# A start-up rearranged: a differently split first conv, w_out's first quarter through SyncE, super 3's input queued early, another order of turns

## The chip, the cores and the metric

The kernel runs on one core of a Trainium2 chip. The metric is the device time in microseconds of one execution, here the median of several. Five engines work side by side: TensorE (PE, with its weight loads PEld), VectorE (DVE), ScalarE (ACT), GpSimd (POOL) and SyncE (SP). [...] DMAs are issued by POOL, ACT and SP, each with a queue of its own.

## The reference

`x` is (8, 4096, 192) f32, `weight` (8, 7), `w_in` (192, 2048), `w_out` (2048, 192). A causal depthwise conv of 7 taps, whose taps are a softmax for each of 8 heads, is followed by a two-layer network with ELU:

```python
w = softmax(weight, axis=-1)                        # (8 heads, 7 taps)
x_pad = concatenate([zeros((B, 6, D)), x], axis=1)
att[b, s, h, g] = sum_k w[h, k] * x_pad[b, s + k, h, g]
h = att.reshape(32768, 192) @ w_in                  # (32768, 2048)
g = where(h > 0, h, exp(minimum(h, 0)) - 1)
out = g @ w_out                                     # (32768, 192)
```

## The kernel before

**Tiling.** The 32768 tokens are 32 "supers" of 1024 tokens, and a super is two groups of 512 tokens, one for each half of TensorE's rows (r or g = 0, 1; 64 rows each, the two halves run side by side). The 192 channels are three tiles of 64 (j = 0, 1, 2). The 2048 hidden units are 16 blocks of 128 (q). A "unit" (n, r) is one hidden block of one group: three matmuls H (L1029) fill one PSUM bank of 128 x 512; ACT takes the exponential out of it into `E` (L756); POOL clips it to at most 1 (L710); DVE takes `max(E - 1, H)`, which is the ELU, into `gT` (L866) and so frees the bank. The second product O (L1052) then runs with gT as weights and `w_out` as the moving side, into accumulators that ACT copies to `osb` (L763), which SP stores. There are eight banks, shared by units, accumulators and convs.

**The conv.** For supers 1 to 31 it is a banded matmul (L1004): windows of x, loaded by POOL into `xg` (L627), times `Tm`, a band of taps; ACT copies the result to `csb` (L752), and SP transposes it by DMA into `att` (L608). `Tm` is made once: DVE writes `wband` (L822), SP writes it to DRAM as `conv_band` (L1075), waits for that to land, and reads it back with a skewed pattern (L1084).

**The first super** takes another way, since nothing is loaded yet. ACT loads all its x to `xs` by one DMA; PE transposes it (L936), ACT and DVE copy it to `xT` (L740, L830), and a conv of tap matmuls (L978) makes the three parts of `att`: each matmul is a diagonal of taps, 64x64, times xT shifted by the tap. Four such 64x64 quarters of TensorE can run at once: the tiles j = 0 and j = 2 use the two diagonal quarters, j = 1 the other two. Of tile 0's seven taps, `ON_DVE` = 3 are done on DVE instead (L837, L842) and added at the end (L849). Tile 2 is done in two halves of 256 columns, in two banks; ACT copies the first to `att` (L744), DVE the second (L851). Only then do the first H matmuls run.

**Weights.** POOL's queue issues, in this order: `w_in` in two column halves of three DMAs each (L647; cast to bf16 on the way), the first piece of `w_out` (L658, blocks 0 to 3, cast to fp16 on the way), both groups of x of super 1 (L627), two more pieces of w_out (blocks 4 to 7, 8 to 15), both groups of x of super 2, and the first group of x of super 3; then its clips begin. The second group of super 3 is issued before clip number 48 (`X3_AT`). `w_in` lands on partitions 0 to 63 and is copied to 64 to 127 for the other row half: ACT copies two parts (L734) and DVE two (L854) from the first column half, ACT a third one later, and SP the rest by DMA (L1092).

**Order.** PE's order is planned while the program is built: `live` (L232) runs the first 16 hidden blocks through a model of the engines (constants `ACT_H`, `POOL_H`, `DVE_H`, `TURNS`, times `LANDS` at which loads are there, `UPPER_LATE` at which the second row half may begin) and always issues what can begin first; `emit` (L189) merges fixed lists after that. The order is a list that PE follows strictly: a matmul whose semaphore has not come holds everything behind it. ACT's and DVE's orders follow from PE's. The engines' own instruction streams are in order too.

The core of the merge of the first conv, and the wait that each O matmul has on its piece of w_out:

```python
rows_of = [
    [(0, tap, 0, GS, 0) for tap in range(KSIZE - ON_DVE)]
    + [(2, t, GS // 2 * c, GS // 2 * (c + 1), 2 + c) for c in range(2) for t in range(KSIZE)],
    [(1, tap, 0, GS, 1) for tap in range(KSIZE)],
]
...
W(s_w[2 + next(k for k in range(1, 4) if q < WOUT[k])], 16)
```

Of the kernel before, what the change touches and what calls it, by code (L numbers as in the profile page):

```python
# [6 lines left out]
ACT = mybir.ActivationFunctionType  # L7
# [3 lines left out]
FP32 = mybir.dt.float32  # L11
# [23 lines left out]
O_AT = (12, 16)  # L35
CONV_AT = (14, 18, 22, 26)
CONV_POS = ((4, 4), (4, 4), (4, 4), (4, 4))
POS_FROM = 19
QB = 2
WARM = (8, 1, 4)  # L40
WCOLS = ((0, 8 * FC), (8 * FC, 16 * FC))
UPPER = ((0, FC), (FC, 2 * FC), (2 * FC, 4 * FC), (4 * FC, 8 * FC), (8 * FC, 16 * FC))
WOUT = (0, 4, 8, 16)
X3_AT = (0, 48)
HALO = 8
BW = P
ON_DVE = 3
XL = GS - CW * (NWIN - 1) + PAD
XI = SUP // P
MM_H, MM_O, MM_C = 216.0, 82.5, 102.5  # L50
# [7 lines left out]
LATE_Q, COPY_AT = 9, 6  # L58
LIVE, UNTIL = 16, 20
EARLY_O = (4, 8)  # L60
LANDS = {"x": {1: 7200.0, 2: 14200.0}, "w_in": 10200.0, "w_out": (3900.0, 8400.0, 11000.0)}
DONE_PE, TO_ACT, TO_POOL, TO_DVE, TO_PE = 165.0, 40.0, 85.0, 35.0, 60.0
ACT_H, ACT_C, ACT_O, POOL_H, DVE_H = 495.0, 470.0, 390.0, 578.0, 600.0
ENDS_ACT, ENDS_POOL, ENDS_DVE, TRANSPOSED = 103.0, 37.0, 84.0, 5000.0
TURNS = 320.0
X_AT = ((2, 1, 1), (1, 1, 0))
ZERO_AT = 8
TAIL = 18
UPPER_LATE = 600.0


def bass_lightweight_conv__then__act_elu_kernel(
# [159 lines left out]
    def live(last, convs, turns):  # L232
# [26 lines left out]
        def o_ready(rt, g):  # L259
            if not turns[rt][g]:  # L260
                return far
            k, q0, q1, visit, *_ = turns[rt][g][0]
            if visits.get((k, g), 0) != visit:
                return far
            t = max(gt_at.get((NQ * (k // 2) + q, g), far) for q in range(q0, q1))
            if k < 2:
                t = max(t, LANDS["w_out"][next(i for i in range(3) if q1 <= WOUT[i + 1])])
            if visit == 0:
                return max(t, min(freed))
            return max(t, turned[k, g])  # L270
# [143 lines left out]
    with ExitStack() as stack:  # L414
# [39 lines left out]
        block8 = sbuf("block8", [HEADS, HEADS, KSIZE], BF16)  # L454
        wband = sbuf("wband", [P, HEADS + 1, BW], BF16)
        scr = sbuf("scr", [P, 2], FP32)
        H = psum("H", [P, NBANK, GS])

        s_wq = sema("s_wq")
# [8 lines left out]
        s_xs = sema("s_xs")  # L468
        s_xh = sema("s_xh")
        s_wb = sema("s_wb")  # L470
        s_xz = sema("s_xz")
        s_cast = sema("s_cast")
        s_tap = sema("s_tap")
# [51 lines left out]
        def att_need(s):  # L525
# [7 lines left out]
            ("t", 3): (0, 2),  # L533
            ("d", 0): (0, 3),
            ("d", 1): (3, 0),
            ("d", 2): (4, 4),
        }

        def first_evacuated(W, what):
# [74 lines left out]
        def _gpsimd(g: bass.BassGpSimd):  # L614
# [78 lines left out]
            ).then_inc(s_id)  # L693
            load_w_in(0)
            load_w_in(1)
            load_w_out(0)
            for gr in range(2):
                load_x(1, gr)
            load_w_out(1)
            load_w_out(2)  # L700
            for gr in range(2):
                load_x(2, gr)
            for i, (n, u) in enumerate(units):
# [15 lines left out]
        @block.scalar  # L719
        def _scalar(a):  # L720
            W = Waits(a)
            a.dma_start(
                xs[:, :, :], x_flat[0:SUP, :].rearrange("(p i) d -> p i d", i=XI)
            ).then_inc(s_xs, 16)
            a.memzero(scr[:, 0:1]).then_inc(s_scr)  # L725
            W(s_scr, 1)
            a.activation(scr[:, 1:2], scr[:, 0:1], ACT.Exp)
            W(s_set, 2)
            a.activation(wex[:], wq2[:], ACT.Exp).then_inc(s_wex)
            W(s_xs, 16)  # L730
            for j in (0, 2):
                a.activation(*cast(j), ACT.Copy).then_inc(s_cast)  # L732
            def upper_half(c0, c1):
                a.activation(  # L734
                    w_in[HP:P, :, c0:c1], w_in[0:HP, :, c0:c1], ACT.Copy
                ).then_inc(s_wa)

            for j in range(1, 3):
                W(s_xt, 2 * j)
                a.activation(*transposed(j), ACT.Copy).then_inc(s_fa)  # L740
            W(s_first[1], 1)
            a.activation(*first_att(1, 0, GS), ACT.Copy).then_inc(s_fa)
            W(s_first[2], 1)
            a.activation(*first_att(2, 0, GS // 2), ACT.Copy).then_inc(s_fa)  # L744
            W(s_w[0], 48)
            for k in range(2):
                upper_half(*UPPER[k])
            for item in act_order:
                if item[0] == "c":
                    m = item[1]  # L750
                    W(s_cv, m + 1 - CU)
                    a.activation(*conv_evac(W, m), ACT.Copy).then_inc(s_ce)  # L752
                elif item[0] == "h":
                    i = unit_at[item[1:]]
                    W(s_h, i + 1)
                    a.activation(  # L756
                        E[:, i % NE, :], H[:, bank_of[item], :], ACT.Exp
                    ).then_inc(s_exp)
                    if i == COPY_AT:
                        W(s_w[1], 48)  # L760
                        upper_half(UPPER[4][0], FC * LATE_Q)
                else:
                    a.activation(*out_evac(W, *item[1:]), ACT.Copy).then_inc(s_oev[item[2]])  # L763
            evacuated_by(W, NK - 1, 1)
            out_group(a, NK - 1, 1)

        @block.vector
        def _vector(v):
# [79 lines left out]
            to, at = first_att(0, 0, GS)  # L848
            v.tensor_tensor(to, at, part[:], ALU.add).then_inc(s_fd)  # L849
            W(s_first[3], 1)  # L850
            v.tensor_copy(*first_att(2, GS // 2, GS)).then_inc(s_fd)  # L851
            W(s_w[0], 48)
            for c0, c1 in UPPER[2:4]:
                v.tensor_copy(w_in[HP:P, :, c0:c1], w_in[0:HP, :, c0:c1]).then_inc(s_wc)  # L854
            for item in dve_order:
                if item[0] == "e":
                    v.tensor_copy(*out_evac(W, *item[1:])).then_inc(s_od)  # L857
                    continue
                _, n, u = item
                i = unit_at[n, u]  # L860
                s, q = divmod(n, NQ)
                if s >= NG3:
                    for g in range(2):
                        W(s_fin[g], 2 * (s - NG3 + 1))
                W(s_clp, i + 1)
                v.scalar_tensor_tensor(  # L866
                    out=gT[:, s % NG3, q, u, :],
                    in0=E[:, i % NE, :],
                    scalar=1.0,
                    in1=H[:, bank_of[item], :],  # L870
                    op0=ALU.subtract,
                    op1=ALU.max,
                ).then_inc(s_tt)

        @block.tensor
        def _tensor(pe):
# [19 lines left out]
            for item in pe_order:  # L896
# [58 lines left out]
                elif item[0] == "d":  # L955


                    rows_of = [
                        [(0, tap, 0, GS, 0) for tap in range(KSIZE - ON_DVE)]
                        + [(2, t, GS // 2 * c, GS // 2 * (c + 1), 2 + c) for c in range(2) for t in range(KSIZE)],  # L960
                        [(1, tap, 0, GS, 1) for tap in range(KSIZE)],
                    ]
                    merged, ends = [], [0, 0]
                    while any(rows_of):
# [6 lines left out]
                    for j, tap, c0, c1, which in merged:  # L971
# [2 lines left out]
                            W(s_tap, 3)  # L974
                        last = KSIZE - 1 - (ON_DVE if j == 0 else 0)
                        for r in range(2):
                            rows, to = half_of(r), half_of(r ^ (j == 1))
                            ins = pe.matmul(  # L978
                                H[to, bank_of["d", j] + (j == 2 and c0 > 0), c0:c1],
                                taps[rows, tap, rows],  # L980
# [58 lines left out]
                else:  # L1039
# [6 lines left out]
                        wait_bank(("a", k, g))  # L1046
                    if visit is not None and not opens:
                        W(s_turn[g], turns[k, g])
                    W(s_w[2 + next(k for k in range(1, 4) if q < WOUT[k])], 16)
                    W(s_tt, tt_count(NQ * t + q, g))  # L1050
                    t0 = 2 * P * half + P * kb
                    ins = pe.matmul(  # L1052
# [14 lines left out]
        def _sync(sy):  # L1067
# [3 lines left out]
                weight[:, :],  # L1071
            ).then_inc(s_wq, 16)
            sy.dma_start(xh[:, :], x_flat[GS - HALO : GS, :]).then_inc(s_xh, 16)
            W(s_tap, 3)
            sy.dma_start(  # L1075
                bass.AP(
# [57 lines left out]
```

## Time and profile before

| what | value |
|---|---|
| median of 4 runs | 718.27 us (718.07 to 718.58) |
| profiled execution | 718.58 us, its span 716.8 us |
| granted TensorE clock | 1.00 throughout |
| H matmuls (L1029) | 3072, 64x512 each |
| O matmuls (L1052) | 8192, 64x192 each |
| banded conv (L1004) | 496, 64x240 each |
| gT on DVE (L866) | 1024, mean 682 ns |
| clip on POOL (L710) | 1024, mean 614 ns |
| exponential on ACT (L756) | 1024, mean 601 ns |
| HBM read, written | 34.63 MB, 25.46 MB |

The time of the profiled execution is 1.8 us more than its span, which begins with the program's first instruction. A mean duration is longer than the spacing of instructions that follow each other, since the next one starts before the last has drained: clips of 614 ns mean start some 575 ns apart. "Busy" for PE means that at least one matmul is in its pipeline, so a stage in which PE is busy all the time can still hold far fewer matmuls than another; the counts of the stages tell that.

### The profile page before, as it was taken

How to read it: one execution, taken by the hardware profiler on the slowest of the kernel's cores; microseconds unless marked ns; L12 is line 12 of the kernel's file. 1: busy time of each engine (PE TensorE's matmuls, PEld its weight loads, DVE VectorE, ACT ScalarE, POOL GpSimd, SP SyncE). 2: the span in 40 equal slices, each digit the busy share in tenths (PEclk: the TensorE clock that was granted, in tenths of full speed). 3: DMA queues.
4: the chain of work that ended last, by engine and by line, in shares of the span. 5: the costliest groups of instructions: out<-in, count | busy, mean ns of one | idle time of the engine just before them, and what ended most of it. 6: DMA issues, size and time to landing. Idle time of an engine off the chain costs nothing.

```text
span 716.8 us, 27665 instructions
## 1 busy us (share of the span) xinstructions
PE 710.8 (99%) x11875; PEld 681.8 (95%) x11875; DVE 642.0 (90%) x1048; ACT 677.3 (95%) x1290; POOL 663.7 (93%) x1112
## 2 busy tenths in 40 slices
PE   8999999999999999999999999999999999999998
PEld 4689999999999999999999999999999999999998
DVE  7999899998898998899998989988989988999994
ACT  6999999999999999999999999999999999999994
POOL 9999999999999999999999999999999999999893
PEclk9999999999999999999999999999999999999999
DMA  9635334564443554444654344544445534434212
GB/s 185 97 72 93 67 73 77 93 87 75 80 80 74 94 90 64 77 86 80 87 90 71 72 77 95 87 73 77 84 73 91 93 63 76 89 81 84 58 48 69
DMA packets 132303, 58.80 MB, mean 82 GB/s; under 512 B 98374, under 2 KB 131412, under 8 KB 132180
## 3 DMA queue, kind: packets, MB, share of 16 engines
q0 software_dynamic: 43504, 16.77, 22.7%
q1 hardware_dynamic: 88388, 39.37, 22.3%
q8 instruction: 93, 1.52, 0.9%
q10 hardware_dynamic: 288, 0.88, 0.4%
q14 instruction: 30, 0.25, 0.1%
HBM read 34.63 MB, written 25.46 MB: 84 GB/s over the span
## 4 chain that ended last, share of the span: by engine, by line
PE 96%; POOL 2%; ACT 1%; DVE 0%; issue 0%; DVEq 0%; POOLq 0%
PE H L1052 54%; PE H L1029 37%; PE H L1004 4%; POOL xg L627 1%; ACT E L756 1%; POOL w_in L647 1%; POOL E L710 1%; POOL w_out L658 0%; DVE gT L866 0%; ACT csb L752 0%; POOL owner L675 0%; DVE osb L857 0%; POOL block L685 0%; POOL ident L664 0%; POOL ones L662 0%
## 5 line engine op out<-in xcount | busy, mean ns | idle before, releaser
L866 DVE SCALAR_TENSOR_TENSOR gT<-E,H 128x512 f16<-128x512 f32 x1024 | 631.9, 682 | 62.1 <-POOL E L710 57.6
L1029 PE MATMUL H<-att,w_in 64*128 64x512 bf16 x3072 | 679.8, 376 | 1.4 <-DVE gT L866 1.0
L1052 PE MATMUL H<-w_out,gT 64*128 64x192 f16 x8192 | 680.5, 243 | 0.1
L710 POOL TENSOR_SCALAR E<-E 128x512 f32<-128x512 f32 x1024 | 603.1, 614 | 41.2 <-ACT E L756 34.3
L1052 PEld LDWEIGHTS H<-w_out,gT 64*128 64x128 f16 x8192 | 606.4, 94 | 17.7 <-PE H L1052 1.5
L756 ACT ACTIVATE E<-H 128x512 f32<-128x512 f32 x1024 | 585.0, 601 | 24.0 <-PE H L1029 0.5
L1029 PEld LDWEIGHTS H<-att,w_in 64*128 64x128 bf16 x3072 | 275.7, 93 | 7.6 <-DVE gT L866 3.0
L1004 PE MATMUL H<-xg,Tm 64*128 64x240 bf16 x496 | 90.9, 263 | 0.0
L752 ACT ACTIVATE csb<-H 112x480 bf16<-112x480 f32 x124 | 70.7, 570 | 0.5 <-PE H L1004 0.3
L763 ACT ACTIVATE osb<-H 128x384 f32<-128x384 f32 (+1 forms) x129 | 62.0, 482 | 6.9 <-PE H L1052 6.8
L627 POOL DMA_DIRECT2D xg<-in_x_dram x62 | 55.0, 900 | 0.2 <-issue 0.2
L1004 PEld LDWEIGHTS H<-xg,Tm 64*128 64x128 bf16 x496 | 42.6, 94 | 1.2 <-DVE gT L866 0.3
L857 DVE COPY osb<-H 128x192 f32<-128x192 f32 x1 | 0.4, 357 | 7.3 <-PE H L1052 7.3
L903 PE MATMUL H<-const-bfloat16-1.0 128*128 128x512 bf16 x12 | 4.5, 535 | 0.8 <-PEq L1119 0.8
L903 PEld LDWEIGHTS H<-const-bfloat16-1.0 128*128 128x128 bf16 x12 | 1.3, 124 | 2.8 <-issue 2.5
L647 POOL DMA_DIRECT2D w_in<-in_moe_w_in_dram x6 | 3.8, 660 | 0.0
L732 ACT ACTIVATE xb<-xs 128x512 bf16<-128x512 f32 x2 | 1.1, 621 | 2.4 <-DMA xs<-in_x_dram 2.4
L658 POOL DMA_DIRECT2D w_out<-in_moe_w_out_dram x3 | 3.0, 1058 | 0.0
L978 PE MATMUL H<-xT,taps 64*64 64x256 bf16 (+1 forms) x50 | 2.6, 317 | 0.0
L978 PEld LDWEIGHTS H<-xT,taps 64*64 64x64 bf16 x50 | 2.0, 106 | 0.5
L725 ACT ACT_TABLE_LOAD x1 | 1.3, 1283 | 1.2 <-PEq L1119 1.2
L936 PEld LDWEIGHTS H<-ident,xb 64*64 64x64 bf16 x48 | 1.2, 127 | 1.3 <-ACT xb L732 1.2
(44 smaller groups left out, 20.9 us busy)
## 6 DMA issues: line engine op xcount, KB each, us to landing
out_dram<-osb SPq DMA_DIRECT2D x126, 192.0 KB, 2.9
xg<-in_x_dram POOLq DMA_DIRECT2D x61, 240.0 KB, 4.6
xs<-in_x_dram ACTq DMA_DIRECT2D x1, 768.0 KB, 4.6
w_in<-in_moe_w_in_dram POOLq DMA_DIRECT2D x6, 128.0 KB, 4.3
att<-csb SPq DMA_TRANSPOSE x31, 3.9
w_out<-in_moe_w_out_dram POOLq DMA_DIRECT2D x2, 192.0 KB, 7.9
w_out<-in_moe_w_out_dram POOLq DMA_DIRECT2D x1, 384.0 KB, 11.8
w_in<-w_in SPq DMA_DIRECT2D x1, 336.0 KB, 6.7
```

The costliest lines, as they stand in the source:

```text
L627: g.dma_start(xg[0:rows, b, 2 * w0 + gr : 2 * w1 : 2, :], src).then_inc(s_x[b][gr], 16)
L647: g.dma_start(w_in[0:HP, j, c0:c1], bass.AP(tensor=moe_w_in.tensor, offset=8 * j * FF + c0, ap=[[CPH * FF, HEADS], [FF, 8], [1, c1 - c0]], ...
L710: g.tensor_scalar(out=E[:, i % NE, :], in0=E[:, i % NE, :], scalar1=1.0, scalar2=0.0, op0=ALU.min, op1=ALU.max,).then_inc(s_clp)
L752: a.activation(*conv_evac(W, m), ACT.Copy).then_inc(s_ce)
L756: a.activation(E[:, i % NE, :], H[:, bank_of[item], :], ACT.Exp).then_inc(s_exp)
L763: a.activation(*out_evac(W, *item[1:]), ACT.Copy).then_inc(s_oev[item[2]])
L866: v.scalar_tensor_tensor(out=gT[:, s % NG3, q, u, :], in0=E[:, i % NE, :], scalar=1.0, in1=H[:, bank_of[item], :], op0=ALU.subtract, op1=A ...
L903: pe.matmul(H[:, bank, :], nc.const_aps.tensor(1.0, (P, P), BF16), nc.const_aps.tensor(1.0, (P, GS), BF16), start=True, stop=True,)
L978: ins = pe.matmul(H[to, bank_of["d", j] + (j == 2 and c0 > 0), c0:c1], taps[rows, tap, rows], xT[rows, j, HALO - PAD + tap + c0 : HALO - P ...
L1004: ins = pe.matmul(H[:, bank_of["c", m], 256 * q : 256 * q + UC], Tm[rows, h, :], xg[rows, s % NXB, :, CPH * h : CPH * (h + 1)].rearrange(" ...
L1029: ins = pe.matmul(H[:, bank_of[item[:3]], :], w_in[HP * r : HP * (r + 1), j, FC * q : FC * (q + 1)], att[HP * r : HP * (r + 1), s % 2, j, ...
L1052: ins = pe.matmul(acc_of(k, g)[:, D * kb : D * (kb + 1)], gT[HP * rt : HP * (rt + 1), t % NG3, q, g, t0 : t0 + P], w_out[HP * rt : HP * (r ...
```

## The change

Six edits, all in the first 50 us of the kernel:

- The first conv: two taps on DVE instead of three; tile 2 is cut at column 352 (`SPLIT`) instead of 256, and its last 160 columns run on the quarters of tile 1 (so its row halves arrive swapped, and DVE copies them back in two instructions of 64 rows).
- ACT's two copies of w_in's upper half come before its copies of `att`, not after.
- w_out's blocks 0 to 3 are loaded by SP as f32 into a new buffer `wo`, after x has landed and ahead of `conv_band`; DVE casts them into `w_out` after its two w_in copies and ahead of its first gT. O matmuls of these blocks wait for the cast (`s_wo`). Blocks 4 to 15 come as one DMA by POOL.
- Both groups of super 3's x are issued before POOL's first clip.
- Constants of the planner: landing times, POOL_H and DVE_H, TURNS, and UPPER_LATE from 600 to 1200.
- `POS_FROM`: the convs of blocks 17 and 18 take the later positions too.

```diff
-POS_FROM = 19
+POS_FROM = 17
-WOUT = (0, 4, 8, 16)
-X3_AT = (0, 48)
+WOUT = (0, 4, 16)
+X3_AT = (0, 0)
-ON_DVE = 3
+ON_DVE = 2
+SPLIT = 352
-LANDS = {"x": {1: 7200.0, 2: 14200.0}, "w_in": 10200.0, "w_out": (3900.0, 8400.0, 11000.0)}
+LANDS = {"x": {1: 7200.0, 2: 14200.0}, "w_in": 10200.0, "w_out": (3600.0, 9700.0)}
-ACT_H, ACT_C, ACT_O, POOL_H, DVE_H = 495.0, 470.0, 390.0, 578.0, 600.0
+ACT_H, ACT_C, ACT_O, POOL_H, DVE_H = 495.0, 470.0, 390.0, 570.0, 590.0
-TURNS = 320.0
+TURNS = 250.0
-UPPER_LATE = 600.0
+UPPER_LATE = 1200.0
...
             load_w_in(0)
             load_w_in(1)
-            load_w_out(0)
             for gr in range(2):
                 load_x(1, gr)
             load_w_out(1)
-            load_w_out(2)
...
+            W(s_w[0], 48)
+            for k in range(2):
+                upper_half(*UPPER[k])
             W(s_first[1], 1)
             a.activation(*first_att(1, 0, GS), ACT.Copy).then_inc(s_fa)
             W(s_first[2], 1)
-            a.activation(*first_att(2, 0, GS // 2), ACT.Copy).then_inc(s_fa)
-            W(s_w[0], 48)
-            for k in range(2):
-                upper_half(*UPPER[k])
+            a.activation(*first_att(2, 0, SPLIT), ACT.Copy).then_inc(s_fa)
...
-            v.tensor_copy(*first_att(2, GS // 2, GS)).then_inc(s_fd)
+            to, at = first_att(2, SPLIT, GS)
+            for g in range(2):
+                v.tensor_copy(
+                    to[HP * g : HP * (g + 1), :], at[HP * (1 - g) : HP * (2 - g), :]
+                ).then_inc(s_fd)
             W(s_w[0], 48)
             for c0, c1 in UPPER[2:4]:
                 v.tensor_copy(w_in[HP:P, :, c0:c1], w_in[0:HP, :, c0:c1]).then_inc(s_wc)
+            W(s_w[3], 16)
+            v.tensor_copy(w_out[:, 0 : WOUT[1], :], wo[:, :, :]).then_inc(s_wo)
...
-                        + [(2, t, GS // 2 * c, GS // 2 * (c + 1), 2 + c) for c in range(2) for t in range(KSIZE)],
-                        [(1, tap, 0, GS, 1) for tap in range(KSIZE)],
+                        + [(2, tap, 0, SPLIT, 2) for tap in range(KSIZE)],
+                        [(1, tap, 0, GS, 1) for tap in range(KSIZE)]
+                        + [(2, tap, SPLIT, GS, 3) for tap in range(KSIZE)],
...
-                            rows, to = half_of(r), half_of(r ^ (j == 1))
+                            rows, to = half_of(r), half_of(r ^ (which % 2))
...
-                    W(s_w[2 + next(k for k in range(1, 4) if q < WOUT[k])], 16)
+                    if q < WOUT[1]:
+                        W(s_wo, 1)
+                    else:
+                        W(s_w[4], 16)
...
             sy.dma_start(xh[:, :], x_flat[GS - HALO : GS, :]).then_inc(s_xh, 16)
+            W(s_xs, 16)
+            sy.dma_start(
+                wo[:, :, :],
+                moe_w_out.rearrange("(q p) d -> p q d", p=FC)[:, 0 : WOUT[1], :],
+            ).then_inc(s_w[3], 16)
             W(s_tap, 3)
```

## The prediction

> **What bounds the kernel now.** I read the page first. TensorE is busy for 99% of the span at the full granted clock, and matmuls are 91% of the chain that ended last.
>
> ```profile
> span 716.8 us, 27665 instructions
> PE 710.8 (99%) x11875; PEld 681.8 (95%) x11875; DVE 642.0 (90%) x1048; ACT 677.3 (95%) x1290; POOL 663.7 (93%) x1112
> PE H L1052 54%; PE H L1029 37%; PE H L1004 4%; POOL xg L627 1%; ACT E L756 1%; POOL w_in L647 1%; POOL E L710 1%; POOL w_out L658 0%; DVE gT L866 0%; ACT csb L752 0%; POOL owner L675 0%; DVE osb L857 0%; POOL block L685 0%; POOL ident L664 0%; POOL ones L662 0%
> ```
>
> Busy time hides the start-up, so I read the busy time by stage next (each engine's busy us with its count of instructions in brackets; PE is the first).
>
> ```profile
> 24.00:28.00 4.00, 3.95 (x40) 2.16 (x37) 3.62 (x6) 4.00 (x10) 3.43 (x6) 1.00 0.27 49
> 28.00:32.00 4.00, 4.00 (x47) 2.35 (x46) 4.00 (x8) 3.93 (x9) 3.92 (x8) 1.00 0.43 68
> 36.00:40.00 4.00, 4.00 (x62) 3.35 (x62) 3.86 (x7) 3.87 (x9) 3.76 (x7) 1.00 0.15 49
> 60.00:80.00 20.00, 20.00 (x344) 19.17 (x339) 18.50 (x31) 19.27 (x38) 18.87 (x33) 1.00 0.43 83
> ```
>
> From 60 us on PE finishes 344 matmuls in 20 us, 69 per 4 us; between 24 and 32 us it is called busy too, yet finishes 40 and 47. So PE is the bound only from about 36 us. Before that it is another engine; the timeline of the first microseconds names the chain that starts it (start, duration, then in brackets the idle time and its releaser).
>
> ```profile
> 5.93 1.12 POOL L658 DMA_DIRECT2D w_out<-in_moe_w_out_dram  x1
> 6.72 2.04 POOL L627 DMA_DIRECT2D xg<-in_x_dram  x2
> 8.55 1.84 POOL L658 DMA_DIRECT2D w_out<-in_moe_w_out_dram  x2
> 10.17 2.78 POOL L627 DMA_DIRECT2D xg<-in_x_dram  x3
> 12.78 1.41 POOL L710 TENSOR_SCALAR E<-E 128x512 f32<-128x512 f32 x2
> 13.64 2.48 DVE L866 SCALAR_TENSOR_TENSOR gT<-E,H 128x512 f16<-128x512 f32 x4 [1.03 <-POOL E L710]
> 14.39 1.49 PE L1029 MATMUL H<-att,w_in 64*128 64x512 bf16 x7 [0.87 <-DVE gT L866]
> ```
>
> The first exponential on ACT runs from 11.45 for 0.60 us, so E is there at 12.05; POOL is still writing DMA descriptors and clips it only at 12.78. DVE starts its gT at 13.64, and PE, out of banks, waits 0.87 us. After that VectorE alone, in the windows of L866, is busy 21.94 of 22.5 us from 13.5 to 36 us: it makes 40 gT at some 0.6 us each, back to back. A shift of its first gT is therefore a shift of everything up to 36 us, and from there PE carries the same shift to the end. Two other places matter: SyncE's queue, and a hole at 43 us.
>
> ```profile
> 6.77 0.37 SPq L1075 DMA_DIRECT2D conv_band<-wband  x1
> 12.67 0.35 SPq L1084 DMA_DIRECT2D Tm<-conv_band  x1
> conv_band<-wband SPq DMA_DIRECT2D x1, 288.0 KB, 5.9
> Tm<-conv_band SPq DMA_DIRECT2D x1, 256.0 KB, 5.6
> 19.26 0.26 PE L1004 MATMUL H<-xg,Tm 64*128 64x240 bf16 x1
> 42.80 0.89 POOL L627 DMA_DIRECT2D xg<-in_x_dram  x1
> 44.38 1.88 DVE L866 SCALAR_TENSOR_TENSOR gT<-E,H 128x512 f16<-128x512 f32 x3 [0.76 <-POOL E L710]
> 45.12 0.39 PE L1029 MATMUL H<-att,w_in 64*128 64x512 bf16 x1 [0.18 <-DVE gT L866]
> ```
>
> Tm lands at 12.67 + 5.6 = 18.3 and the first banded conv reads it at 19.26: 1.0 us of slack. At 42.80 POOL issues the second half of super 3's x; VectorE stands 0.76 us and PE 0.18 us.
>
> [...] the two copies of L854, bf16 in SBUF, take 0.67 and 1.19 us beside POOL's descriptor writing[...] DMA is over 90% busy from 4 to 9 us, and conv_band, 288 KB, needs 5.9 us there. [...]
>
> **The change part by part.** The sums are against the profiled execution, 718.58 us with a span of 716.8; the median is 718.27, and I carry the difference over to it.
>
> *POOL's queue.* Spacings of starts: w_out's first piece 6.72 - 5.93 = 0.79; two xg 1.83; two w_out 10.17 - 8.55 = 1.62, so 0.83 for eight blocks; three xg to the first clip 2.61. Sum 6.85. After: two xg 1.83, one piece of twelve blocks 0.87 (the slope from four to eight), four xg 4 x 0.87 = 3.48, sum 6.18. POOL is free at 5.93 + 6.18 = 12.1, just as E is ready: gain up to 0.65 us at the first clip.
>
> *VectorE's queue.* One tap less: -0.75 (L842). The 128x256 copy (0.42) becomes two of 64x160, 0.3 each by that row: +0.2. L854 then ends near 12.4 instead of 12.61. New after it: wait for wo, then cast 768 columns. wo is issued near 5.5, once xs has landed (ACT's first read of it is at 5.46). Landing: conv_band's 5.9 or the first w_out's 7.3 us later, so 11.4 to 12.8; I take 12.4. Everything on VectorE, so every gT, queues behind this wait. The cast: 0.72 us by scaling L814 (512 columns in 0.48)[...]; I take 0.6. If it does not collide, gT starts at 12.1 + 0.83 + 0.05 = 13.0, or at 13.0 by VectorE's own queue. If cast and clip exclude each other, 12.1 + 0.83 + 0.6 = 13.55. [...] I take 13.55: gain 0.1, bounds +0.6 and -0.3.
>
> *First conv.* Each diagonal pair has 5 x 512 + 7 x 352 = 5024 columns instead of 4 x 512 + 7 x 512 = 5632; 608 columns at 216 ns per 512 (PE's spacing) end it 0.26 us sooner, at 10.1. But the first H needs all three parts of att, and ACT now makes two w_in copies first (L734, 0.93 us). The third w_in transfer, issued at 3.8, lands near 9.2, so the copies end at 10.1, att(1) at 10.65 and 352 columns of att(2) at 11.05; the third H started at 10.97 before. Gain nothing: the copies that stood after att now stand before it.
>
> *SyncE's queue.* wo (128 x 4 x 192 x 4 B = 393 KB) now lies ahead of conv_band. The same bytes crossed the same engines at that time before, so the least cost is nothing; the most is its own passage at the 200 GB/s of 10 to 12 us, 2.0 us. I take 0.8: Tm lands near 19.1, inside the slack. At 2.0 the first conv would wait 1.0 to 1.1 us with all H and O behind it. xl and w_in's upper half (lands near 21.0) move as much; its first reader, unit 9, runs at 22.2, so it is covered when Tm is.
>
> *w_out's rest.* Twelve blocks now land as one, about when the last piece did (9.3 + 11.8 = 21.1). O of q = 4 stood 76th in PE's order and stands 91st, which before was at 21.2. Cost 0 to 0.5; I take 0.1.
>
> *Super 3's x.* The issue at 42.80 goes. VectorE's hole of 0.76 closes; PE's visible idle is 0.18 us, its first O after it a little later too: gain 0.3 (0.2 to 0.4). Its transfer is now queued with the others, up to some 25 us, where the transpose of att (issued 25.82) may share engines with it; H of super 1 starts at 30.9, a microsecond after that transpose lands.
>
> *Order of turns.* From the middle of unit 18 to the end all engines' orders are the same, bank numbers apart; the steady state and the tail are not touched.
>
> Sum: -0.1 - 0 + 0.1 - 0.3 = -0.3 us: 718.3 for the profiled one, 718.0 on the median.
>
> **The rivals.**
> - [...] gT starts at 13.0: -0.6 - 0.3 = -0.9, with a shorter startup order up to -1.4: 716.9 to 717.4. For it: E is ready at 12.05 and POOL at 12.1. Against: the slow L854 copies.
> - *The SyncE queue decides.* wo delays Tm by 2.0 us or more and w_in's upper half with it: first conv +1.1 to +1.8, gT +0.3 for a late wo, -0.3 for the hole: 719.4 to 720.1, slower. It decides from 1.0 us of delay on. For it: conv_band already needs 5.9 us for 288 KB. Against: those bytes were in the way before.
> - *VectorE waits for wo.* Tm in time, but wo at 13.2, as w_out's first piece (5.93 + 7.3): gT at 13.9 to 14.2: +0.3 to +0.6 - 0.3 + 0.1: 718.4 to 718.7.
>
> **How the numbers follow.** Likeliest case 0.47 (718.0, its own range 717.4 to 718.6), no collision 0.2, SyncE's queue 0.2, wo late 0.13. 0.2% is 1.44 us, about what a measurement of this kernel tells from no change: limits 716.83 and 719.71. Only the far end of the second case (0.12) and most of the third (0.16) lie outside. Range 716.8 to 719.7.
>
> **What would show it.** POOL's first clip near 12.2; first gT at 13.0 (no collision), 13.55 or 13.9; VectorE idle before the w_out cast, if wo is late; conv_band and Tm landings, and idle PE before the first L1004 matmul; no VectorE hole at 43 us; 344 matmuls in 60 to 80 us again. A change of that last count would make the whole argument wrong.

## The result and the profile after

| | before | after |
|---|---|---|
| median | 718.30 us (62 runs, 718.01 to 719.34) | 721.32 us (42 runs, 718.62 to 724.77) |
| ratio, 95% interval | | 1.0045, 1.0036 to 1.0054: 0.45% slower, beyond the noise |
| profiled execution, its span | 718.58 us, 716.8 us | 718.85 us, 716.9 us |

The median stands where hardly any execution is: the 42 times of the changed kernel lie in two groups of 21, from 718.6 to 720.8 and from 721.9 to 724.8 us, most of the second above 723.3. The kernel before, run beside it, has no second group (62 runs up to 719.34). The mean granted clock splits the same way: it is 0.999 or 1.00 in every run of the lower group and 0.993 to 0.998 in every run of the upper one. The profiled execution belongs to the lower group; a profile of the upper one came from running the same kernel again (724.51 us, span 722.7 us). The two are the same program, so what differs between them is most of the loss. A smaller part is in both: the lower group's median, 719.25 us, is already 0.95 us above that of before, and the profiled 718.85 is among its fastest.

The ratios here and below lie near the quotient of the mean times, not of the medians. With two groups these can differ: in `e1_again`, below, the means give 1.0049 and the medians 1.0070.

First the windows view of the changed kernel in its lower execution, then in its upper one (the columns are the stretch, its length, each engine's busy us with its count of instructions, PE first, then PEld, DVE, ACT, POOL, the granted clock, the DMA share and GB/s).

```profile
12.00:16.00 4.00, 4.00 (x30) 1.40 (x26) 3.74 (x7) 3.92 (x8) 3.66 (x7) 1.00 1.51 217
16.00:20.00 4.00, 3.91 (x42) 2.09 (x40) 4.00 (x7) 3.81 (x8) 4.00 (x8) 1.00 1.41 250
20.00:24.00 4.00, 3.99 (x49) 2.52 (x46) 3.71 (x7) 3.77 (x8) 3.27 (x6) 1.00 1.53 206
24.00:28.00 4.00, 4.00 (x52) 2.66 (x47) 3.33 (x7) 4.00 (x9) 3.16 (x7) 1.00 0.64 97
60.00:80.00 20.00, 20.00 (x341) 19.35 (x338) 18.47 (x30) 19.31 (x37) 18.87 (x33) 1.00 0.44 84
80.00:100.00 20.00, 20.00 (x344) 19.49 (x341) 18.12 (x30) 19.24 (x38) 18.80 (x32) 1.00 0.48 88
```

```profile
12.00:16.00 4.00, 1.84 (x14) 0.61 (x11) 1.77 (x1) 3.95 (x8) 4.00 (x8) 0.99 1.51 215
16.00:20.00 4.00, 2.59 (x11) 0.88 (x11) 4.00 (x7) 1.24 (x3) 1.65 (x3) 0.50 1.51 221
20.00:24.00 4.00, 3.84 (x28) 2.00 (x28) 3.34 (x7) 1.80 (x4) 2.02 (x4) 0.50 1.43 235
24.00:28.00 4.00, 4.00 (x43) 2.81 (x40) 2.20 (x4) 2.73 (x7) 2.02 (x4) 0.73 0.39 46
60.00:80.00 20.00, 20.00 (x342) 19.43 (x337) 18.01 (x30) 19.24 (x38) 19.12 (x33) 1.00 0.50 88
```

Between 12 and 28 us PE finishes 30 + 42 + 49 + 52 = 173 matmuls in the one and 14 + 11 + 28 + 43 = 96 in the other, and VectorE makes 28 instructions against 19. From 60 us on they keep the same pace (341 and 342 matmuls in 60 to 80 us, 344 before). The loss is made before 28 us, and a part of it at half the clock. The timeline of VectorE says where it starts; the first two lines are the lower execution, the next two the upper one, and the last one of each fence is the first gT.

```profile
12.98 0.56 DVE L861 CAST w_out<-wo 128x768 f16<-128x768 f32 x1 [0.26 <-DMA wo<-in_moe_w_out_dram]
13.47 1.27 DVE L873 SCALAR_TENSOR_TENSOR gT<-E,H 128x512 f16<-128x512 f32 x2
```

```profile
14.23 2.52 DVE L861 CAST w_out<-wo 128x768 f16<-128x768 f32 x1 [2.33 <-DMA wo<-in_moe_w_out_dram]
16.68 3.66 DVE L873 SCALAR_TENSOR_TENSOR gT<-E,H 128x512 f16<-128x512 f32 x6
```

The same cast of 768 columns, waiting for the same transfer: in one execution wo lands at 12.96 and the cast takes 0.56 us; in the other it lands at 14.21 and the cast takes 2.52. The first gT stands behind it. PE has filled its banks by then in the upper execution (2 + 22 H matmuls, three to each of eight banks):

```profile
10.87 2.96 PE L1038 MATMUL H<-att,w_in 64*128 64x512 bf16 x22 [0.17 <-DVE att L854]
17.41 2.31 PE L1038 MATMUL H<-att,w_in 64*128 64x512 bf16 x8 [3.57 <-DVE gT L873]
```

PE idles for 3.57 us, and the clock records show 0.5 from 15.91 for 10.24 us. In the lower execution PE has no gap above 0.25 us between 11 and 24 us and no such record. At 718.58 + 3.04 (the first gT at 16.68 instead of 13.64) the upper execution would be at 721.6; the other 2.9 us of its 724.51 follow with the halved clock.

SyncE's queue shows the second effect, in the DMA issues of the lower execution (KB, then us from issue to landing):

```profile
wo<-in_moe_w_out_dram SPq DMA_DIRECT2D x1, 384.0 KB, 7.4
conv_band<-wband SPq DMA_DIRECT2D x1, 288.0 KB, 7.1
Tm<-conv_band SPq DMA_DIRECT2D x1, 256.0 KB, 5.2
```

conv_band takes 7.1 us where it took 5.9, and lands at 14.03 instead of 12.66; Tm lands at 19.26 instead of 18.28. The first banded conv starts at 19.30, on Tm's heels.

### The profile page after: what moved, and what is told of

Same layout as the page of the kernel before. It is cut to its first block, busy times and chain, and to the rows that moved or that the text cites. A ratio compares the mean times of both kernels' runs of the same rounds, so it can differ in the third digit from the quotient of the medians.

```text
span 716.9 us, 27669 instructions
## 1 busy us (share of the span) xinstructions
PE 712.6 (99%) x11877; PEld 681.4 (95%) x11877; DVE 642.0 (90%) x1049; ACT 677.9 (95%) x1290; POOL 663.1 (92%) x1110
## 4 chain that ended last, share of the span: by engine, by line
PE 97%; DVE 2%; ACT 0%; issue 0%; POOL 0%; DVEq 0%
PE H L1064 55%; PE H L1038 37%; PE H L1013 4%; DVE gT L873 1%; PE H L910 1%; ACT E L757 0%; DVE part L838 0%; ACT csb L753 0%; DVE xT L831 0%; DVE part L843 0%; PE H L943 0%; DVE att L850 0%; POOL E L711 0%; DVE osb L864 0%; PE H L920 0%
## 5 line engine op out<-in xcount | busy, mean ns | idle before, releaser
L987 PE MATMUL H<-xT,taps 64*64 64x512 bf16 (+2 forms) x52 | 2.3, 319 | 0.0
```

The lines of the kernel that those rows point to most:

```text
L987: ins = pe.matmul(H[to, bank_of["d", j] + (j == 2 and c0 > 0), c0:c1], taps[rows, tap, rows], xT[rows, j, HALO - PAD + tap + c0 : HALO - P ...
```

## The experiments

No kernel below leaves out a part of the computation; some write a buffer that nothing reads, and say so. A row of the later table is one profiled execution, while times and ratios are medians over all runs of a kernel.

### Which part of the change loses the time

`e1_again` is the changed kernel as it is.

> The changed kernel again, to see whether its times stay spread between 718.6 and 724.8 us in two groups (about 719.2 and 724), and to have a second profile of it. Theory X3 (the early transfer of super 3's second x group runs into the first transpose of att): two groups again, and a profile from the upper group would show the first H of super 1 some 5 us late behind L611's transpose. Theory W (twelve blocks of w_out as one transfer land with no slack before O of q = 4): two groups too, but the 5 us stand before that O, near 22 us. Theory T (Tm late behind wo): the 5 us stand before the first L1013 matmul, near 19 us.

723.67 us (718.99 to 724.99), ratio 1.0048 (1.0031 to 1.0064). It repeats the loss and the two groups, ten of 17 runs above 722, and gave the upper profile shown above. None of the three places that the theories name is where the time is lost: that is ahead of the first gT.

`e1_no_wo` has everything of the change except wo:

```diff
+            load_w_out(0)
...
-            W(s_w[3], 16)
-            v.tensor_copy(w_out[:, 0 : WOUT[1], :], wo[:, :, :]).then_inc(s_wo)
...
-            W(s_xs, 16)
-            sy.dma_start(
-                wo[:, :, :],
...
```

> The changed kernel with w_out's blocks 0 to 3 loaded by POOL with a cast as before (first after w_in), no wo, no cast on DVE, SyncE's queue as before. Theory T: the upper group vanishes and the first L1013 no longer waits for Tm; near 718.5. Theories X3 and W: two groups remain.

718.78 us (718.54 to 719.33), ratio 1.0003 (0.9995 to 1.0011): no difference from before, and one group. First conv, order of turns, early x and two pieces of w_out together cost and bring nothing that can be told.

`e2_before_wo` is the other side, wo alone added to the kernel before.

> The kernel before with one part of the change alone: w_out's first quarter by SyncE into wo, cast on VectorE ahead of the first gT. POOL's first clip comes 0.8 us sooner (12.0). Theories P and L: this part alone brings the two groups and a median of 720 to 724. If another part of the change is needed as well: near 718.3.

721.32 us (719.03 to 722.32, 6 runs), ratio 1.0037 (1.0025 to 1.0049). wo alone brings most of the loss (0.37 of 0.45%), though no time above 722.4. In its profile wo lands at 14.37, the cast takes 1.02 us and PE idles for 2.67.

Two runs moved super 3's x, first out of the change and then alone into the kernel before (`X3_AT = (0, 48)` and `(0, 0)`).

> The changed kernel with the second x group of super 3 issued before clip 48 again, nothing else. Theory X3: the upper group vanishes, one group near 718.7 (the hole at 43 us is back, about 0.3 us on the lower group's 719.2, or 719.5). Theories W and T: two groups remain, median above 720.

720.23 us (718.87 to 722.99), ratio 1.0026 (1.0017 to 1.0035). About half of the loss is left, and no time is above 723.0, where nine of e1_again's 17 are: POOL is free before the first exponential here, and the profiled cast, though wo landed at 13.79, took 0.95 us.

> The kernel before with both groups of super 3's x issued ahead of the first clip, nothing else. Theory X3: two groups appear here as well, or a rise of some 3 us in the median. Theories W and T: one group near 718.3, at most 1 us later because POOL's first clip waits for one more descriptor write (0.9 us).

719.36 us (719.01 to 721.90), ratio 1.0017 (1.0010 to 1.0024). Alone, early x costs: POOL issues four loads where it issued three, and the timeline of that run has the first clip at 13.95, 1.17 us later than before.

```profile
10.34 3.60 POOL L627 DMA_DIRECT2D xg<-in_x_dram  x4
13.95 1.22 POOL L710 TENSOR_SCALAR E<-E 128x512 f32<-128x512 f32 x2
```

PE's gap grows from 0.87 to 1.71 us, and the clock is halved for 3.41 us from 17.20 (this profile is one of seven of the 21 runs with a mean clock under 0.999; the other 14 lie between 719.0 and 719.5). In the change two pieces of w_out merged into one and w_out's first piece gone from POOL pay for this.

### Which property of wo's path

Four runs take one property away each. `e2_cast_act` moves the cast to ScalarE, behind its fifth exponential, so that VectorE waits for nothing new and only SyncE's queue is different:

```diff
-            W(s_w[3], 16)
-            v.tensor_copy(w_out[:, 0 : WOUT[1], :], wo[:, :, :]).then_inc(s_wo)
...
+                if i == 4:
+                    W(s_w[3], 16)
+                    a.activation(w_out[:, 0 : WOUT[1], :], wo[:, :, :], ACT.Copy).then_inc(s_wo)
```

> The changed kernel with the cast of wo on ACT after its fifth exponential, so no wait and no cast ahead of VectorE's first gT; the load by SyncE stays. Theories P and L: VectorE's first gT near 13.0 to 13.2 in every run, no upper group, 718.0 to 719.0. Theory X3 or T (the early x or the late Tm stretches the run): the upper group stays.

719.55 us (719.29 to 722.04), ratio 1.0023 (1.0014 to 1.0032): slower than the 718.0 to 719.0 expected, with a mean clock of 0.998 in three of 11 runs. The first gT is at 13.67, as before but not at the 13.0 to 13.2 expected (the first exponential starts only at 12.33; `e3_wo_early`, below, shows why), and PE has no gap near it. What is left is Tm, which lands at 20.45; PE's timeline:

```profile
20.04 0.24 PE L1067 MATMUL H<-w_out,gT 64*128 64x192 f16 x1
20.50 0.27 PE L1016 MATMUL H<-xg,Tm 64*128 64x240 bf16 x1 [0.21 <-DMA Tm<-conv_band]
```

The first banded conv is 1.24 us later than before (19.26), and the median 1.2 us higher than that of the runs of before beside it (718.37); a cast of 0.87 us on ScalarE is in that as well.

`e2_cast_reduce` leaves everything in place and makes the cast by `tensor_reduce` with a maximum over an axis of one element, an instruction with the same result.

> The changed kernel with the cast of wo done by a VectorE reduction over an axis of one element, at the same place behind the same wait, in place of the copy. Theory P ([...]2.52 us instead of 0.57 in e1_again, once wo lands after the first clips have begun): the cast takes 0.8 to 1.0 us wherever it starts, the first gT is at wo's landing + 1 us, and most of the upper group goes: median 719 to 720. Theory L (only the late landing of wo matters, the queue wait of 2.3 us): nothing gained, two groups as in the changed kernel, median above 721.

719.85 us (718.52 to 722.21), ratio 1.0023 (1.0016 to 1.0029). No run of 21 lies above 722.3, where nearly half of the changed kernel's are. The reduction takes 0.95 us, within the 0.8 to 1.0 of theory P, by which the clips keep the copy waiting (2.52 us in the upper execution) and not the reduction.

`e3_wo_early` drops one line, SyncE's wait for x ahead of wo (`W(s_xs, 16)`).

> The changed kernel, but SyncE issues wo's load at once instead of after x has landed (near 2.5 instead of 5.5 us). Theory A (the loss comes from wo landing after POOL's clips have begun[...], PE idle, its clock halved): wo lands by 11 us, the cast lasts 0.5 to 0.8 us and ends before 12.6, first gT by 13.1, no halved clock after the start; all runs lie together, 717.5 to 719.0 us, none above 721. x, which wo now travels beside, may land up to 0.8 us later and take that from the gain. Rival B (SyncE's queue decides: 384 KB ahead of conv_band cost what they cost wherever they stand): conv_band still lands after 14 us and the runs above 723 us stay.

718.84 us (718.25 to 720.21), ratio 1.0008 (1.0000 to 1.0016): the upper group is gone. wo lands at 7.54, and the cast lies ahead of the first clip. VectorE's timeline:

```profile
10.65 1.25 DVE L859 COPY w_in<-w_in 64x768 bf16<-64x768 bf16 x2
11.94 0.69 DVE L861 CAST w_out<-wo 128x768 f16<-128x768 f32 x1
13.73 6.73 DVE L873 SCALAR_TENSOR_TENSOR gT<-E,H 128x512 f16<-128x512 f32 x11 [1.11 <-POOL E L711]
```

conv_band still lands at 14.32 and Tm at 19.67. So the queue's delay stays while the large loss goes; they are two things, and the queue's is small.

The first gT missed its forecast: 13.73 instead of 13.1, though the cast was done at 12.62. The reason is another part of the change. ACT's two w_in copies now stand ahead of its copies of att, and in this run the third w_in transfer landed only at 9.99 (9.13 before, 8.46 in the lower execution). That wo now travels beside it is shown only in part as the reason: w_in's first transfer landed at 7.64 here and between 6.1 and 6.7 elsewhere, but the third came at 9.92 in `e2_cast_act` too. ACT waits for it, and PE for ACT:

```profile
10.01 0.93 ACT L735 ACTIVATE w_in<-w_in 64x384 bf16<-64x384 bf16 x2 [1.57 <-DMA w_in<-in_moe_w_in_dram]
11.62 1.62 PE L1038 MATMUL H<-att,w_in 64*128 64x512 bf16 x11 [1.17 <-ACT att L746]
```

So the first exponential starts at 12.40, 0.95 us later than before. The same wait, of 0.4 to 0.9 us, stands in six other profiles with the changed first conv, those in which this transfer landed at 9.26 or later; in the five in which it landed by 8.80 it is absent.

`e3_cast_third` puts wait and cast behind the first two gT.

> The changed kernel, but VectorE's wait for wo and its cast stand behind the first two gT instead of ahead of them. POOL's clips then run when the cast starts, whatever wo's landing. Theory A[...]: the cast lasts well over 0.6 us (1.2 to 3) and ends just as a run of clips ends. Theory A', lateness: the first gT is at 13.0 to 13.3, so two banks come free and PE's first gap is under 0.5 us; but PE has to stand later, when the cast is stretched: 719 to 722 us. Rival B (the 2.52 us cast was slow from the DMA's writes into SBUF and not from the clips): the cast lasts 0.6 us here too in runs in which wo has landed earlier, and the time is 718.3 to 718.9 us.

720.05 us (718.51 to 722.56), ratio 1.0027 (1.0014 to 1.0040). The first gT is at 13.35, but the cast, started at 14.59 amid clips, takes 0.93 us, not the 1.2 to 3 that I expected of any cast amid clips; and PE stands three times: for 0.86 us for att, as in `e3_wo_early`, for 0.70 us for a gT behind the cast, and for 0.64 us for Tm, which lands at 20.65. The delay is moved, not saved, and my account of what a cast meets amid clips was too coarse.

### What a late first gT costs by itself

Two kernels have neither wo nor cast: before, with a write of an unread buffer on VectorE ahead of the first gT (`v.memset(late[:], 0.0)`, 3500 and 1300 columns).

> The kernel before with one VectorE memset of 3500 columns (about 3.6 us, of which 1.0 lie in its idle time) into an unused buffer ahead of the first gT, nothing else: it makes gT start near 16.3 instead of 13.64, the work asked for is otherwise the same. Theory C [...]: about 2.7 us from the lateness and 1 to 4 more from the clock, 721.5 to 725, with a clock record of 0.5 after 15 us. Without C: 718.65 + 2.7 = 721.3 in every run, clock 1.00.

722.78 us (721.83 to 723.02), ratio 1.0056 (1.0043 to 1.0069).

> The kernel before, with a write of a new buffer late of 128x1300 f32 on VectorE ahead of its first gT: the same delay as in the run with 3500 columns, but shorter (1300/3500 of its length, some 1.3 us of which 0.4 fall into VectorE's waiting). Theory A (a late first gT passes on one to one, and a PE gap of 3 us costs more on top since the clock is halved afterwards): first gT near 14.4, PE's gap near 1.6 us, no halved clock or one in some runs only; 719.0 to 719.5 us, less than one third of the 4.4 us that 3500 columns cost. Rival B (only the lateness counts, no clock): the cost is proportional to the delay of the first gT, 4.4 x 0.8/3.26 = 1.1 us: 719.5, and all runs lie together.

718.97 us (718.39 to 720.39), ratio 1.0010 (1.0002 to 1.0018). The delay came out smaller than the 0.8 us expected: the profiled execution has its first gT 0.38 us late (14.02) and lies 0.38 us over that of before. With 3500 columns the first gT is 3.26 us late (16.90) and the execution 4.35 us longer. The extra 1.1 us comes with a halved clock of 3.41 us. The other profiles say the same. The table sets each against the profile of before; the clock goes with PE's longest gap after the first conv (four more profiles, with gaps under 0.9 us and the full clock, are left out).

| run | first gT | later by | PE's longest gap | clock at 0.5 for | execution longer by |
|---|---|---|---|---|---|
| after, lower | 13.47 | -0.17 us | 0.34 us | none | 0.27 us |
| e2_cast_reduce | 14.43 | 0.79 | 0.83 | none | 0.91 |
| before | 13.64 | | 0.87 | none | |
| e1_x3_late | 14.69 | 1.05 | 1.03 | none | 1.31 |
| e3_dve_late_short | 14.02 | 0.38 | 1.15 | none | 0.38 |
| e3_wo_early | 13.73 | 0.09 | 1.17 | none | 0.26 |
| e4_loose | 14.66 | 1.02 | 1.60 | 3.41 us | 2.28 |
| e1_before_x3_early | 14.63 | 0.99 | 1.71 | 3.41 | 2.29 |
| e4_packed_reduce | 15.70 | 2.06 | 1.81 | 6.83 | 4.34 |
| e2_before_wo | 15.33 | 1.69 | 2.67 | 3.41 | 3.08 |
| e2_dve_late | 16.90 | 3.26 | 3.41 | 3.41 | 4.35 |
| e1_again, upper | 16.68 | 3.04 | 3.57 | 10.24 | 5.93 |
| e4_packed | 17.38 | 3.74 | 4.44 | 10.24 | 6.23 |

In the rows with the full clock an execution is 0 to 0.44 us longer than its first gT is late; with one piece of half clock it is 1.1 to 1.4 us longer, with two 2.3, with three 2.5 and 2.9. (Of the four profiles left out, `e1_no_wo` lies at 0; three lie 0.9 to 1.3 us above, and in these PE waits later, for Tm or w_out.) The plainest pair is `e1_x3_late` and `e4_loose` (`e1_x3_late` with one wait more, which was over by then): first gT at 14.69 and 14.66, and 0.97 us between their times, with a piece of half clock in the longer one.

### Why one cast takes 2.5 us and the others one

In the upper execution 8 clips follow each other from 12.24 on. In others the clips run through as well, yet the cast gets in after one clip. The difference in the traces is how densely they follow: in the upper one each of the first seven exponentials had been ready 0.3 to 0.7 us before its clip, and each clip starts 0.07 us, later 0.04, before the one ahead has ended. Elsewhere the first clips waited for their exponentials (each starts 0.08 to 0.1 us after one), and later ones overlap by 0.02 to 0.04. Three runs force the cases, with the cast made to wait for the third clip. In the packed ones POOL writes an unread buffer of 800 columns ahead of its clips (the first edit below), so that exponentials pile up; in the loose one super 3's x is late instead, so that POOL is free first.

```diff
+            g.memset(pad[:], 0.0)
             for i, (n, u) in enumerate(units):
...
             W(s_w[3], 16)
+            W(s_clp, 3)
             v.tensor_copy(w_out[:, 0 : WOUT[1], :], wo[:, :, :]).then_inc(s_wo)
```

> The changed kernel with super 3's second x late (POOL is free before the first exponential, clips follow ACT), and VectorE's cast made to wait for the third clip as well. Theory A (packed clips shut the cast out, loose ones let it in at the next boundary): the cast starts near 14.4, waits out one clip and ends 0.9 to 1.05 us after its start. Rival B (any run of clips shuts it out until the run ends): 2 us or more. Rival C (nothing to do with clips, DMA writes slow it down): 0.57 to 0.7 us, or at random.

> The changed kernel with a write of a new buffer pad of 128x800 f32 on POOL ahead of its clips, so that exponentials are there before the clips, and VectorE's cast made to wait for the third clip as well. Theory A: clips start 0.57 us apart with 0.07 us of overlap from the first on, the cast starts near 15 and ends only behind the last clip that finds its exponential ready (the 7th or 8th): 2 to 3 us; PE idles 3 us or more, and the time is over 723 us. Rival B (any run of clips): the same, with the loose run just as long. Rival C: 0.57 to 1.05 us.

> As the packed run, but the cast is a reduction by maximum over an axis of one element. Theory A [...]: 0.96 us as before, beside the same packed clips, first gT near 16. Rival (VectorE or SBUF is slow there for another reason): stretched as the copy is, 2 us or more.

The VectorE timelines, loose, packed, and packed with the reduction:

```profile
13.91 0.82 DVE L862 CAST w_out<-wo 128x768 f16<-128x768 f32 x1 [2.05 <-DMA wo<-in_moe_w_out_dram]
14.66 5.46 DVE L874 SCALAR_TENSOR_TENSOR gT<-E,H 128x512 f16<-128x512 f32 x9
```

```profile
14.86 2.60 DVE L864 CAST w_out<-wo 128x768 f16<-128x768 f32 x1 [2.26 <-POOL E L713]
17.38 3.07 DVE L876 SCALAR_TENSOR_TENSOR gT<-E,H 128x512 f16<-128x512 f32 x5
```

```profile
14.83 0.95 DVE L864 TENSOR_REDUCE w_out<-wo 128x768 f16<-128x768 f32 x1 [2.25 <-POOL E L713]
15.70 4.86 DVE L881 SCALAR_TENSOR_TENSOR gT<-E,H 128x512 f16<-128x512 f32 x8
```

And POOL's timeline of the packed run:

```profile
12.88 5.04 POOL L713 TENSOR_SCALAR E<-E 128x512 f32<-128x512 f32 x8
20.29 0.61 POOL L713 TENSOR_SCALAR E<-E 128x512 f32<-128x512 f32 x1 [2.36 <-ACT E L759]
```

The packed cast starts at 14.86 and ends at 17.46, inside the eighth clip (16.94 to 17.92, where a clip of this run otherwise takes 0.7 us and overlaps the next by 0.1), behind which POOL has nothing to do. The reduction starts at the same time amid equally packed clips and takes 0.95 us, and no clip beside it is longer than its neighbours. So it is the copy (2.60 us), not the same cast as a reduction (0.95 us), that this packed stream of clips kept out, and it kept it out through several clips, where the loose stream let it in after one (0.82 us). In all seven profiles with a copying cast beside clips, one clip takes 0.25 to 0.32 us more than its neighbours, and the cast ends 0.40 to 0.52 us after that clip has started: the rest of its time is waiting. That holds for the 0.56 us of the lower execution too, whose cast happened to start 0.15 us before a clip ended. In both packed executions the cast gets in as the eighth clip begins, the last of the run, and not behind it as forecast. Clips overlap there by 0.04 us in the upper one and 0.10 in the forced one, hardly less than at the places before it; so the overlap alone doesn't say where it gets in, and what lets it in there stays open.

The times are 722.01 us for the loose run (ratio 1.0054, 1.0034 to 1.0074), 724.18 for the packed one (1.0081, 1.0052 to 1.0110) and 722.92 for the reduction (1.0063, 1.0040 to 1.0085), with two to four runs each. All four loose executions have a mean clock below 1 (0.995 in three, and 0.998 in the profiled one, with its 3.41 us at 0.5; against six of 19 below 0.998 in `e1_x3_late`), so their median says little of the cast. The packed run is the upper group made on purpose, with its gap, its clock and its time.

### Is there a version that beats both

`e3_no_wo_x3_late` keeps the first conv and the order, without wo and with late x.

> Differs from the changed kernel in two things: w_out's blocks 0 to 3 come from POOL with the cast in flight as before (no wo, no VectorE cast, SyncE's queue as before), and super 3's second group of x is issued before clip 48 as before. Theory A (the loss is all of wo's path; early x has two sides, a late first clip of some 0.9 us and a closed hole of 0.3 us): POOL is free one descriptor writing, 0.9 us, earlier than without the late x, the first clip near 12.1, first gT near 13.0, ratio 0.9985 to 0.9995, 717.3 to 718.0 us. Rival B (the first clip waits for E anyway or VectorE's two copies decide): first gT stays at 13.6, 718.4 us, ratio 1.000. Rival C (early x was a pure gain here): 718.7 to 719.1 us, since the hole at 43 us comes back.

718.63 us (718.15 to 719.77), ratio 1.0005 (0.9997 to 1.0013). The first gT is at 13.00, 0.64 us earlier than before, as expected, and the time is the same. PE's timeline shows where it is given back:

```profile
22.14 0.24 PE L1063 MATMUL H<-w_out,gT 64*128 64x192 f16 x1 [0.85 <-DMA w_out<-in_moe_w_out_dram]
```

The one large w_out load lands at 22.00, and the O that needs it first now waits for 0.85 us. None of the versions beats the kernel before.

## Why the prediction was wrong

The forecast was 718.0 us with 716.8 to 719.7; 721.32 was measured. Its steps one by one:

- **VectorE's queue: the step that failed.** It took wo's landing for 12.4 and the cast for 0.6 (the author's estimate; scaling L814 gave 0.72), with 13.55 for the first gT and 13.9 as the latest. Ten profiles with wo in this place show it landing between 12.96 and 14.37. The lower execution's first gT, 13.47, is near the forecast by luck: wo landed earliest there, and the cast met the end of a clip. The cast took 0.56 us in one, 0.82 to 1.02 in four, and over 2.5 in the two in which clips were packed. The first gT came at up to 16.68 in the changed kernel. That cast and clip might exclude each other was in the prediction as an assumption, counted as one cast that delays one clip; that a late cast can stand behind a whole run of clips (2.52 us in the upper execution) was not.
- **A cost that no step had: the clock.** The sum carried a late gT to the end one to one. The table shows that this holds within 0.44 us while the clock stays full and PE waits for nothing else later, and that each execution with a halved clock is 1.1 to 2.9 us longer than that (the two write runs: 0.38 us longer for 0.38, 4.35 for 3.26). The records of half clock last 3.41, 6.83 or 10.24 us, that is one, two or three times 3.41. Gaps of 1.60 to 1.81 us already came with one or two such pieces, and in the 3.41 us just ahead of `e4_loose`'s half clock PE was busy for 2.44, so that execution did not need an idle PE for all of that time.
- **SyncE's queue: right place, wrong size.** Behind wo, conv_band took 7.1 us to land instead of 5.9. 0.8 us of delay for Tm was taken, an estimate, with a point of decision at 1.0. Tm came 1.0 us later in the lower profile and 1.5 to 2.7 us later in the nine others, so it lay beyond that point in all of these but one. With the first gT in time it goes with a cost of 0.5 us (`e3_wo_early`) to 1.2 us (`e2_cast_act`), at its most what the rival "SyncE's queue decides" had; it is the smaller part of the loss.
- **The rival "VectorE waits for wo"** named the wait that decides, and gave it 0.3 to 0.6 us where it took up to 3.0, with 10.24 us of half clock behind it.
- **POOL's queue: right.** Free at 12.1 predicted, 12.21 in the lower profile and 12.24 in the upper one; the four xg DMA_DIRECT2D instructions on POOL, which the prediction calls descriptor writing, took 3.49 us in the lower profile, 3.48 predicted. That very gain packed the clips in the upper one, where the first exponential was there at 11.88.
- **First conv: no gain, as said, but a wait in most profiles.** The tap matmuls took 2.32 us in the lower profile against 2.59 before, close to the 0.26 less that was forecast. The prediction took 9.2 for the landing of the third w_in transfer, on which ACT's copies, and so att and the third H, now wait. In twelve profiles with this first conv it landed between 8.01 and 9.99. In seven of them, from 9.26 on, PE stands 0.4 to 1.2 us in its first H, and the first exponential starts at 11.67 to 12.40 (11.45 before). In four of the other five it starts at 11.12 to 11.28, and three of these four have packed clips (`e1_again`, `e4_packed` and `e1_no_wo`, which has no cast to be kept out; in `e4_loose` POOL is free earlier). The lower execution (11.83) is the fifth: its third H is at 11.42, where 10.97 was the time before, held up by VectorE's copies of att. No run takes this part out alone, so its cost at the end is not known.
- **w_out's rest: right** in the lower profile (landing at 21.68, PE not kept waiting); with an earlier start it becomes the next bound (landing at 22.00 and a wait of 0.85 us in `e3_no_wo_x3_late`).
- **Super 3's x: the hole went, the gain cannot be seen.** VectorE's timeline has no gap at 43 us, and PE finishes 340 matmuls between 40 and 60 us instead of 332. But early and late x without wo give 718.78 and 718.63 us.
- **Order of turns: right.** 341 and 344 matmuls in 60 to 80 and 80 to 100 us, 344 and 344 before; the 3 are less than the 8 gained in the window ahead of them.

Some figures of the working are off, without deciding anything. VectorE makes 37 gT from 13.5 to 36 us, not 40: the four windows count those across an edge twice. L854's end at 12.4 is more than its own terms give (12.61 - 0.75 + 0.2 = 12.06); 12.72 and 11.90 were measured. From 10 to 12 us the DMAs moved 240 GB/s, not 200. And of the cases only SyncE's, 719.4 to 720.1, reaches beyond the limits, so the shares that it puts outside for two cases don't follow from their ranges.

The range was too narrow for the same reason that the sum was wrong: a landing that varies by 1.4 us from run to run was given one value, and the cost behind it was taken as linear.

Open is why wo's landing varies so much (x, for which it waits, landed between 5.21 and 5.53 in all these profiles), and what brings the half clock, and what makes it last one, two or three pieces: the runs don't separate PE's gap from the thin stream of matmuls around it, nor from the moment at which the gap falls.

## What to carry to other kernels

A wait that is put ahead of a strictly ordered engine's main work has to be priced with the latest landing of its transfer, not the likely one, and with everything behind it; if it can be moved to a time at which nothing depends on it (here one wait less on SyncE, wo at 7.54 us), that is worth trying: the large loss went here (718.84 us, against 723.67 in `e1_again`). Where a copy or cast on VectorE falls beside a dense stream of GpSimd work, try it ahead of that stream, or in another form: here the cast took 2.52 and 2.60 us amid packed clips, 0.69 ahead of them, and 0.95 as a reduction amid them. And a gap of TensorE is not worth its length: in these profiles it went with a stretch of half clock from 1.60 us on, and with 1.1 to 2.9 us of time beyond the delay itself.

## What the hardware showed that was not expected

- A cast of 128x768 on VectorE took 0.69 us ahead of the clips, 0.56 to 1.02 us amid loose clips, 2.52 and 2.60 us amid packed ones; as a reduction it took 0.95 us, in the packed case too.
- In the profiles, half clock came in pieces of 3.41 us (one to three of them) with PE gaps of 1.60 us and more, and not with gaps of 1.17 us and less. Two executions with the same first gT (14.66 and 14.69) lay 0.97 us apart, with one piece and with none.
- One transfer of 384 KB, issued at the same point of the same queue, landed anywhere from 12.96 to 14.37 us after the start; issued 3.9 us earlier, it landed at 7.54.
